# Tile-by-tile in place of pool-by-pool waits at the stage transitions of a transformer block

## The chip, the cores and the metric

The kernel runs on one core of one Trainium2 chip. The metric is device time in microseconds (us) of one execution, as the median of several executions; lower is better. The core has a matrix engine (TensorE, PE in the profile; its weight loads are the row PEld), a vector engine (DVE), an activation engine (ACT), POOL, and SP, which here issues all DMA transfers of the program (every issue on the page stands under SP). In the traces the engines work side by side and stand where they need each other's results (DVE stood 87.5 us in all for the snapshots of ACT, in the page of the kernel before); the built program does this with semaphores. Accumulators lie in PSUM, at the two last transitions in tiles of 128 x 512 float32 or of twice that; the down product's pool has eight of the former, which the built program puts into banks 0 to 7, one each. Everything else lies in SBUF or DRAM.

## The reference

Two sub-blocks behind each other, on 2048 tokens of width 1024, in bfloat16:

```python
x = A_x
h = x + A_ref(layernorm(x), A_wqkv, A_wo)        # linear attention, 32 heads of 32
h2 = h + B_ref(layernorm(h), W_gate, W_up, W_down)
# B_ref: gate = relu(x @ W_gate); up = x @ W_up; (gate * up) @ W_down, width 3584
```

## The kernel before

The kernel multiplies by Strassen's scheme with 7 block products (hence the sums called s, t, hs, tg, tu), and goes through stages: k, v and q products; attention interleaved with the rest of q and the first gate/up products; gate/up in a wide form with accumulators of two banks; the down product, in two halves s = 0 and s = 1. Each stage opens pools of tiles in memory that an earlier stage has closed. The pools at the two last transitions:

```python
    psctx.close()
    abctx.close()
    ps2ctx = ExitStack()
    ps2 = ps2ctx.enter_context(tc.tile_pool(name="ps2", bufs=1, space=PSUM))
    apools = [ps2, ps2ctx.enter_context(tc.tile_pool(name="ps2b", bufs=1, space=PSUM))]
    hhpool = ctx.enter_context(tc.tile_pool(name="hhpool", bufs=1, side="right"))
    prepool = ctx.enter_context(tc.tile_pool(name="prepool", bufs=1, side="right"))
    # ... (cut: the loop over the gate/up units)
            p1()
            if prev:
                prev()
            p2()
            prev = p3
    prev()
    ps2ctx.close()
    mctx.close()

    dpool = ctx.enter_context(tc.tile_pool(name="dpool", bufs=1))
    dwork = ctx.enter_context(tc.tile_pool(name="dwork", bufs=4))
    ps3 = ctx.enter_context(tc.tile_pool(name="ps3", bufs=8, space=PSUM))
```

One gate/up unit, with its three accumulators A, Dp and E. A comes from ps2 and ps2b in turn. `snap` is a copy on ACT; `finish_sum` is the drain of an accumulator, an addition on DVE (its line is L615):

```python
        def finish_sum(ps, m, q):
            gu = mwork.tile([P, 2, SW], BF16, tag="gu", name="gu")
            nc.vector.tensor_tensor(out=gu[:], in0=ps[:], in1=m[:], op=ALU.add)     # L615
            # ... (cut: relu on ACT, product on DVE, store of hh)

        def part1():
            st["A"] = A = apools[k % len(apools)].tile([P, 2, SW], FP32, tag="A", name="A")
            prod(A, 1, True)
            m1 = snap(A)
            Dp = ps2.tile([P, 2, SW], FP32, tag="D", name="Dp")
            prod(Dp, 2, True)
            finish_sum(Dp, m1, 0)

        def part2():
            A = st["A"]
            prod(A, 6, False)
            st["u2"] = snap(A)
            st["E"] = E = ps2.tile([P, 2, SW], FP32, tag="E", name="E")
            prod(E, 5, True)
            prod(A, 7, False)
            finish_sum(E, snap(A), 3)

        def part3():
            A, E = st["A"], st["E"]
            prod(A, 4, False)
            # ... (cut: relu and product of A)
            prod(E, 3, False)
            finish_sum(E, st["u2"], 1)
```

The start of the down product, which needs four one-bank accumulators at a time:

```python
        def prod(accs, lhs, rhs, start, after):
            for half in range(2):
                for tt in TT:
                    for f in range(FD):                                     # FD = 7
                        nc.tensor.matmul(accs[tt][:], ...)                  # L759
                    if half == 1:
                        after(tt)
        # ... (cut)
        accA = [ps3.tile([P, DW], FP32, tag="s", name="accA") for _ in TT]
        prod(accA, h11, b11, True, after(lambda tt: snap(accA[tt], 0, tt, "m1"), m1))

        s3 = h21[:].bitcast(FP16)
        for v in range(2):
            fs = slice(v * FD, (v + 1) * FD)
            nc.vector.tensor_tensor(out=s1[:, fs], in0=h21[:, fs], in1=h22[:, fs], op=ALU.add)
            nc.vector.tensor_tensor(out=s2[:, fs], in0=s1[:, fs], in1=h11[:, fs], op=ALU.subtract)
            nc.vector.tensor_tensor(out=s3[:, fs], in0=h11[:, fs], in1=h21[:, fs], op=ALU.subtract)
        accD = [ps3.tile([P, DW], FP32, tag="s", name="accD") for _ in TT]
        prod(accD, h12, b21, True, after(lambda tt: store(0, tt, accD[tt], m1[tt])))
        # ... (cut: sums t1, t2, then the product of s2 and t2 into accA, and so on)
```

## Time and profile before

| | before |
|---|---|
| time, median of 3 runs | 769.52 us (768.56 to 771.18) |
| profiled span | 768.0 us |
| PE busy | 740.3 us, 96% |
| DVE busy | 482.0 us, 63% |

The busy times from the page of the kernel before (engine, us, share of the span, number of instructions):

```profile
PE 740.3 (96%) x3584; PEld 340.2 (44%) x3584; DVE 482.0 (63%) x868; ACT 321.6 (42%) x593; POOL 6.1 (1%) x44
```

Busy for 96% of the span, PE is what bounds the kernel, so the question for any wait is whether PE stands in it. The timeline of PE before shows where it stood at the two last transitions and in the down product. Columns: start in us, length, engine, source line, what is written and read, how many; in brackets the idle time before and what ended it.

```profile
586.91 1.03 PE L596 MATMUL A<-hn,tu 128*128 128x512 f16 x4
589.03 1.02 PE L596 MATMUL A<-hn,tg 128*128 128x512 bf16 x4 [1.10 <-ACT snap L610]
...
591.62 1.03 PE L596 MATMUL E<-hs,wu 128*128 128x512 f16 x4
594.06 12.25 PE L759 MATMUL accA<-wd,hh 128*128 128x512 bf16 x56 [1.41 <-DVE gu L615]
...
711.12 6.20 PE L759 MATMUL accA<-t,s 128*128 128x512 f16 x28 [0.57 <-DVE t L822]
```

Taken as idle time, these are the only three stops over 0.3 us from 298 us on. The one at 594.06 is the transition from gate/up (L596) to the down product (L759). The chain of waits before, around it (start, us, what), says what PE waited for:

```profile
590.92 1.74 PE E L596 x8
592.66 0.02 issue
592.69 1.24 DVE gu L615
593.92 0.14 issue
594.06 12.25 PE accA L759 x56
```

DVE drained E, the last accumulator of gate/up, for 1.24 us, and only then did the first matmul of accA start, 0.14 us later. But accA does not read E. It waited because its pool lies in the memory of a closed pool.

### The profile page before, as it was taken

To read this page: it belongs to the slowest core of one execution; us is meant where nothing else is said; L and a number is where in the kernel's file an instruction comes from. 1 tells how busy PE (TensorE), PEld (TensorE's weight loads), DVE (VectorE), ACT (ScalarE), POOL (GpSimd) and SP (SyncE) were. 2 spreads that over 40 slices of the span, in tenths; PEclk is the share of its full clock that TensorE was granted. 3 is DMA by queue.
4 is the path that set the end of the run, shared out by engine and by line. 5 is a ranking of instruction groups with operands and counts; after the bars stand their busy time and mean duration, and the time that the engine had idled before them with its cause. 6 is when DMAs were issued, how large, how long until landed. Compare 5 with 4: busy or idle time off the path is not lost.

```text
span 768.0 us, 9610 instructions
## 1 busy us (share of the span) xinstructions
PE 740.3 (96%) x3584; PEld 340.2 (44%) x3584; DVE 482.0 (63%) x868; ACT 321.6 (42%) x593; POOL 6.1 (1%) x44
## 2 busy tenths in 40 slices
PE   5999999999889999999999999999998999999998
PEld 2444555444344444444444444444443444444443
DVE  5997654886896766656474564746545991349632
ACT  4775553877777554444444344444434000000000
POOL 0000000000000000000000000000000000000000
PEclk9999999999999999999999999999999999999999
DMA  9675003089767526154032140130001986971001
GB/s 321 145 138 150 1 1 110 1 186 225 180 154 192 121 63 209 45 152 131 7 87 72 34 131 8 55 103 29 28 7 60 331 261 209 316 256 49 28 27 55
DMA packets 125151, 89.76 MB, mean 117 GB/s; under 512 B 50352, under 2 KB 116912, under 8 KB 124592
## 3 DMA queue, kind: packets, MB, share of 16 engines
q1 hardware_dynamic: 125104, 89.15, 40.9%
q8 instruction: 28, 0.46, 0.2%
q14 instruction: 19, 0.16, 0.1%
HBM read 59.77 MB, written 17.83 MB: 101 GB/s over the span
## 4 chain that ended last, share of the span: by engine, by line
PE 64%; DVE 20%; ACT 8%; DMA 4%; issue 3%; SPq 0%; POOL 0%; DVEq 0%; ACTq 0%
PE A L596 16%; PE accA L759 11%; PE E L596 8%; PE accE L759 6%; PE attn L514 4%; DVE gu L615 4%; PE Aq L280 3%; PE Dp L596 3%; PE Aq L414 2%; PE Eq L280 2%; ACT snap L610 2%; PE Aq L629 2%; PE accD L759 2%; DVE stats L249 2%; DMA hn<-hn 1%
## 5 line engine op out<-in xcount | busy, mean ns | idle before, releaser
L615 DVE TENSOR_TENSOR gu<-E,snap 128x1024 bf16<-128x1024 f32 x48 | 58.7, 1223 | 90.1 <-ACT snap L610 87.5
L610 ACT COPY snap<-A 128x1024 f32<-128x1024 f32 x72 | 72.0, 1008 | 84.1 <-PE A L596 84.1
L759 PEld LDWEIGHTS <-hh 128*128 128x128 bf16 (+1 forms) x560 | 54.7, 98 | 67.7 <-issue 1.9
L617 ACT ACTIVATE gu<-gu 128x512 bf16<-128x512 bf16 x72 | 45.4, 630 | 86.2 <-DVE gu L615 85.9
L759 PE MATMUL accA<-wd,hh 128*128 128x512 f16 (+1 forms) x336 | 73.3, 379 | 1.4 <-DVE gu L615 1.4
L514 PE MATMUL attn<-wo_mem,oT 128*128 128x512 bf16 x256 | 59.3, 385 | 3.4 <-DVE o_sb L494 3.1
L596 PEld LDWEIGHTS <-tg 128*128 128x128 f16 x384 | 37.5, 98 | 49.5 <-issue 5.7
L596 PEld LDWEIGHTS <-tu 128*128 128x128 f16 x384 | 37.6, 98 | 45.3
L618 DVE TENSOR_TENSOR hh<-gu 128x512 bf16<-128x512 bf16 x72 | 30.5, 423 | 38.4 <-ACT gu L617 38.4
L147 ACT COPY u<-Aq 128x512 f32<-128x512 f32 x56 | 32.2, 581 | 44.5 <-PE Aq L280 20.9
L596 PE MATMUL A<-hn,tg 128*128 128x512 f16 (+1 forms) x192 | 49.3, 379 | 1.1 <-ACT snap L610 1.1
L596 PE MATMUL A<-hn,tu 128*128 128x512 f16 (+1 forms) x192 | 49.3, 379 | 0.0
L596 PEld LDWEIGHTS <-wg 128*128 128x128 bf16 x288 | 28.2, 98 | 34.5 <-issue 1.1
L596 PEld LDWEIGHTS <-wu 128*128 128x128 bf16 x288 | 28.2, 98 | 34.0
L514 PEld LDWEIGHTS <-oT 128*128 128x128 bf16 x256 | 25.2, 99 | 36.0 <-issue 8.6
L759 PEld LDWEIGHTS <-s 128*128 128x128 f16 x224 | 21.9, 98 | 27.2 <-issue 0.8
L615 DVE TENSOR_TENSOR gu<-Dp,snap 128x1024 bf16<-128x1024 f32 x24 | 29.3, 1220 | 2.3 <-PE Dp L596 2.3
L280 PEld LDWEIGHTS <-xT 128*128 128x128 bf16 (+1 forms) x192 | 18.6, 98 | 23.9 <-issue 2.4
L767 DVE TENSOR_TENSOR u<-accA,hres 128x512 f32<-128x512 f32 x16 | 10.8, 690 | 28.6 <-PE accA L759 28.1
L494 DVE TENSOR_TENSOR o_sb<-nd,rd 128x384 bf16<-128x384 f32 (+1 forms) x48 | 22.9, 508 | 8.6 <-ACT rd L493 8.3
L516 DVE SCALAR_TENSOR_TENSOR x_res<-attn,x_res 128x512 bf16<-128x512 f32 x32 | 22.0, 688 | 7.7 <-PE attn L514 7.6
L596 PE MATMUL E<-hs,tg 128*128 128x512 f16 x96 | 24.6, 378 | 0.9
(161 smaller groups left out, 1217.5 us busy)
## 6 DMA issues: line engine op xcount, KB each, us to landing
wd<-in_B_W_down_dram SPq DMA_DIRECT2D x16, 896.0 KB, 6.5
hh_dram<-hh SPq DMA_DIRECT2D x72, 128.0 KB, 1.7
wg<-in_B_W_gate_dram SPq DMA_DIRECT2D x14, 512.0 KB, 4.9
wu<-in_B_W_up_dram SPq DMA_DIRECT2D x14, 512.0 KB, 4.9
hh<-hh_dram SPq DMA_DIRECT2D x4, 1792.0 KB, 8.0
x_sb<-in_A_x_dram SPq DMA_DIRECT2D x16, 256.0 KB, 3.8
x_res<-in_A_x_dram SPq DMA_DIRECT2D x16, 256.0 KB, 3.0
h_dram<-x_res SPq DMA_DIRECT2D x16, 256.0 KB, 2.6
```

Source lines behind the costliest of these rows:

```text
L147: nc.scalar.copy(out=snaps[nm, v], in_=A[v][:])
L249: nc.vector.bn_stats(out=stats[:, k, :], in_=x_sb[:, k * NW:(k + 1) * NW])
L280: nc.tensor.matmul(ps[:], lhsT=left[m - 1][:, kc, r + v * P:r + (v + 1) * P], rhs=right[m - 1][:, kc, :], start=(start and kc == 0), stop= ...
L494: nc.vector.tensor_tensor(out=ov[:, c0:c0 + n], in0=ndv[:, :, 0:P].rearrange("p k (h e) -> p k h e", h=HPC), in1=rd[:, 0:n, :].unsqueeze(3 ...
L514: nc.tensor.matmul(ps[:], lhsT=st["oT"][:, c, :], rhs=wo_sb[:, c, j * NW:(j + 1) * NW], start=(c == 0), stop=(c == KC - 1))
L516: nc.vector.scalar_tensor_tensor(out=h_sb[:, j * NW:(j + 1) * NW], in0=ps[:], scalar=1.0, in1=h_sb[:, j * NW:(j + 1) * NW], op0=ALU.mult, ...
L596: nc.tensor.matmul(ps[:, v, :], lhsT=w[v][m - 1][:, kc, :], rhs=left[m - 1][:, kc, :], start=(start and kc == 0), stop=(kc == KH - 1), ski ...
L610: nc.scalar.copy(out=m[:], in_=ps[:])
L615: nc.vector.tensor_tensor(out=gu[:], in0=ps[:], in1=m[:], op=ALU.add)
L617: nc.scalar.activation(out=gu[:, 0, :], in_=gu[:, 0, :], func=ACT.Relu)
L618: nc.vector.tensor_tensor(out=d, in0=gu[:, 0, :], in1=gu[:, 1, :], op=ALU.mult)
L759: nc.tensor.matmul(accs[tt][:], lhsT=lhs[:, half * FD + f, tt * P:(tt + 1) * P], rhs=rhs[half][:, f, :], start=(start and half == 0 and f ...
```

## The change

The intent is that a pool opened in memory of earlier pools no longer waits until all of these are done with. Each of its tiles waits for the users of its own bytes. It is one argument on each pool opened at a transition, on 14 lines in all; the core of the diff:

```diff
-    abpool = abctx.enter_context(tc.tile_pool(name="abpool", bufs=3, space=PSUM, side="right"))
+    abpool = abctx.enter_context(tc.tile_pool(name="abpool", reuse_waits="tile", bufs=3, space=PSUM, side="right"))
# ... (cut: the same for qwork0, qwork1, aops, wpool, tpool, mwork)
-    ps2 = ps2ctx.enter_context(tc.tile_pool(name="ps2", bufs=1, space=PSUM))
+    ps2 = ps2ctx.enter_context(tc.tile_pool(name="ps2", reuse_waits="tile", bufs=1, space=PSUM))
# ... (cut: the same for ps2b, hhpool, prepool, dpool, dwork)
-    ps3 = ctx.enter_context(tc.tile_pool(name="ps3", bufs=8, space=PSUM))
+    ps3 = ctx.enter_context(tc.tile_pool(name="ps3", reuse_waits="tile", bufs=8, space=PSUM))
```

Comparing the two built programs shows that no instruction is added, removed or moved on any engine, apart from those that only wait. At the start of accA the waits change like this (the number is the semaphore value waited for; DVE 747 is the drain of E; DVE 746 is the last read of A by DVE, which ended 0.4 us before that drain began; ACT 575 is the last read of A by ACT):

```
before                                      after
wait alone            DVE 747               -
weights of accA tt=0  POOL 40               no wait
matmul of accA tt=0   ACT 575               no wait
first matmul of tt=3  -                     DVE 746
first matmul of accD tt=1  -                DVE 747
```

The banks of the built program say why: accA's four tiles lie in banks 0, 7, 6 and 5, accD's in 4, 3, 2 and 1. Dp was in 0 and 1, E in 2 and 3, the last A in 4 and 5, the A before it in 6 and 7. Only the second accD tile (bank 3) meets E.

More of the change, by code (lines that the diff above doesn't have):

```diff
@@ L424, in q_unit @@
         return strassen(pspool, qw[-1], mm, fin)
-    with tc.tile_pool(name="qwork0", bufs=2, side="right") as pool:
+    with tc.tile_pool(name="qwork0", reuse_waits="tile", bufs=2, side="right") as pool:
         qw.append(pool)
@@ L432, in block_kernel @@
     q1ctx = ExitStack()
-    qw.append(q1ctx.enter_context(tc.tile_pool(name="qwork1", bufs=2, side="right")))
+    qw.append(q1ctx.enter_context(tc.tile_pool(name="qwork1", reuse_waits="tile", bufs=2, side="right")))
     mctx = ExitStack()
@@ L441, in new_hn @@
     def new_hn(s):
-        aops = mctx.enter_context(tc.tile_pool(name=f"aops{s}", bufs=1))
+        aops = mctx.enter_context(tc.tile_pool(name=f"aops{s}", reuse_waits="tile", bufs=1))
         hnT.append([aops.tile([P, KC, SW], BF16, name=f"hn{s}{i}") for i in range(2)])
@@ L448, in block_kernel @@
     NE = 2 * GP
-    wpool = mctx.enter_context(tc.tile_pool(name="wpool", bufs=2))
+    wpool = mctx.enter_context(tc.tile_pool(name="wpool", reuse_waits="tile", bufs=2))
     wg_v = wg.rearrange("(kc p) (h f) -> p kc h f", p=P, h=2)
@@ L566, in block_kernel @@
     new_hn(1)
-    tpool = mctx.enter_context(tc.tile_pool(name="tpool", bufs=2))
-    mwork = mctx.enter_context(tc.tile_pool(name="mwork", bufs=2))
+    tpool = mctx.enter_context(tc.tile_pool(name="tpool", reuse_waits="tile", bufs=2))
+    mwork = mctx.enter_context(tc.tile_pool(name="mwork", reuse_waits="tile", bufs=2))
     hh0 = []
@@ L704, in block_kernel @@
     ps2ctx = ExitStack()
-    ps2 = ps2ctx.enter_context(tc.tile_pool(name="ps2", bufs=1, space=PSUM))
-    apools = [ps2, ps2ctx.enter_context(tc.tile_pool(name="ps2b", bufs=1, space=PSUM))]
-    hhpool = ctx.enter_context(tc.tile_pool(name="hhpool", bufs=1, side="right"))
-    prepool = ctx.enter_context(tc.tile_pool(name="prepool", bufs=1, side="right"))
+    ps2 = ps2ctx.enter_context(tc.tile_pool(name="ps2", reuse_waits="tile", bufs=1, space=PSUM))
+    apools = [ps2, ps2ctx.enter_context(tc.tile_pool(name="ps2b", reuse_waits="tile", bufs=1, space=PSUM))]
+    hhpool = ctx.enter_context(tc.tile_pool(name="hhpool", reuse_waits="tile", bufs=1, side="right"))
+    prepool = ctx.enter_context(tc.tile_pool(name="prepool", reuse_waits="tile", bufs=1, side="right"))
     hh0 += [hhpool.tile([P, FH, SW], BF16, tag="hh", bufs=4, name="hh") for q in range(4)]
@@ L736, in block_kernel @@
     mctx.close()
-    dpool = ctx.enter_context(tc.tile_pool(name="dpool", bufs=1))
-    dwork = ctx.enter_context(tc.tile_pool(name="dwork", bufs=4))
-    ps3 = ctx.enter_context(tc.tile_pool(name="ps3", bufs=8, space=PSUM))
+    dpool = ctx.enter_context(tc.tile_pool(name="dpool", reuse_waits="tile", bufs=1))
+    dwork = ctx.enter_context(tc.tile_pool(name="dwork", reuse_waits="tile", bufs=4))
+    ps3 = ctx.enter_context(tc.tile_pool(name="ps3", reuse_waits="tile", bufs=8, space=PSUM))
     TT = range(NT)
```

## The prediction

> **What bounds the kernel now.** TensorE. The page gives PE 740.3 us busy of 768.0 (96%), granted clock 1.0 nearly everywhere; DVE has 63%. [...] in the timeline matmuls of 512 columns start every 0.216 us, and from 298 us to the last start at 763.8 us that rhythm breaks visibly only three times: 1.3 us at 589.0 (a snapshot that the last gate/up unit's next product needs), 1.57 us at 594.06 (the step from gate/up to the down product) and 0.7 us at 711.1 (a weight sum on DVE).
>
> **What the change does.** No instruction is added, removed or reordered on any engine; only wait conditions change. By stage transition:
>
> 1. Attention's q work and first gate/up tiles (about 125 to 205 us). Some waits go from PE, ACT, POOL and the DMA queue. None of the idle PE time there ends with one of them: the waits view names DVE results that are data (pq_mem, o_sb, x_res, 1 to 2 us each). Worth 0.
> 2. Gate/up with the wide accumulators (297.8 us). The first matmul no longer waits for all earlier PE work; the timeline shows no gap. Worth 0.
> 3. Down product (594.06 us). Before, accA's first matmul waited for the last DVE addition out of the old accumulators, ACT and POOL. The chain of waits shows: matmuls of E end 592.66, DVE gu 592.69 to 593.92, 0.14 us of passing on, accA 594.06. After, the first accA bank has no such wait; the wait moves to the fourth token tile's first matmul (for a DVE result of 592.3) and to accD (for the addition that ends at 593.92), needed about 597 and 607. So PE goes straight on: start to start falls from 1.79 to 0.22 us, saving 1.57 us, all on the critical path.
>
> **Does it survive?** The loads of wd keep their place in the queue behind the hh stores, so the second half of the first weight block still is issued at about 592.7 and lands at 597.7. PE will want it 28 matmuls after its start, at 592.5 + 6.05 = 598.5: about 0.8 us to spare. The hres loads lose a wait for a store (issued 601.5, after about 597), but DMA is full there (share about 1.0 from 595 to 613), so they land hardly sooner. The tightest DVE result is the first half of t (ready 616.1, needed from about 616.7). The gap at 711 should stay about 0.6 us. So I keep 1.5 us.
>
> **Predicted time.** 769.52 - 1.5 = 768.0 us, range 766.2 to 769.8 (the runs before spread 2.6 us). Faster by over 2%: 0.005; within 2%: 0.99; slower: 0.005.
>
> **What would show it.** In the chain of waits DVE gu no longer stands between E and accA; in the timeline accA starts about 0.2 us after E's last start; the idle time "PE accA <- DVE gu 1.4" leaves the groups; hres issues move 4 us forward; nothing before 592 us moves by 0.3 us; span about 766.5.
>
> **What would make it wrong.** The second wd half arriving after 598.5, so that the gap returns 6 us later as a wait for DMA; t late by some tenths at 617; the 711 us gap growing; or an earlier hidden wait among the SBUF pools that the profile puts down to another engine (another 1 to 2 us before 300 us).

## The result, and the profile after

| | before | after |
|---|---|---|
| first comparison, median (runs) | 769.04 us (4) | 767.48 us (4) |
| ratio of the fast runs, 95% interval | | 0.9981 (0.9962 to 0.9999) |
| profiled span | 768.0 us | 767.3 us |
| last start of E to first start of accA | 1.79 us | 0.22 us |
| first wide gate/up matmul to the end | 470.18 us | 468.48 us |

A ratio compares the fast runs of one kernel with those of the other, so it is not quite the ratio of the medians quoted. By the bar of 2% the time is the same.

The chain of waits after, at the same place:

```profile
590.05 1.89 PE A L596 x8
591.94 1.73 PE E L596 x8
593.67 12.09 PE accA L759 x56
605.75 12.09 PE accD L759 x56
617.84 12.09 PE accA L759 x56
```

The drain of E is no longer in the chain. The timeline after shows it running beside accA:

```profile
592.64 1.03 PE L596 MATMUL E<-hs,wu 128*128 128x512 f16 x4
593.29 4.63 PEld L759 LDWEIGHTS <-hh 128*128 128x128 bf16 x22
593.50 4.70 PE L759 MATMUL accA<-wd,hh 128*128 128x512 bf16 x21
593.71 1.23 DVE L615 TENSOR_TENSOR gu<-E,snap 128x1024 bf16<-128x1024 f32 x1 [0.41 <-PE E L596]
```

The two other stops are still there:

```profile
590.05 1.02 PE L596 MATMUL A<-hn,tg 128*128 128x512 bf16 x4 [1.10 <-ACT snap L610]
```

and the stop at 711 us before is a start-to-start distance of 0.94 us at 710.57 after (0.95 before).

At the last gate/up products this profile is 1.02 us later than the one before. That is not the change. The two programs have the same waits up to the first q matmul, which already came at 125.97 against 125.09 us; from there to the first wide gate/up matmul both took about the same, 172.87 and 172.71 us. The first wide gate/up matmuls, before and after:

```profile
297.81 1.03 PE L596 MATMUL A<-hn,wg 128*128 128x512 bf16 x4
298.84 1.03 PE L596 MATMUL A<-hn,wg 128*128 128x512 bf16 x4
```

So comparisons below use the stretch from the first wide gate/up matmul to the end of the span, which holds the two last transitions and whose start is the same point in every kernel.

### The profile page after: what moved, and what is told of

Read it like the earlier page. It is cut to its first block, busy times and chain, and to the rows that moved or that the text cites. A ratio compares the mean times of both kernels' runs of the same rounds, so it can differ in the third digit from the quotient of the medians.

```text
span 767.3 us, 9604 instructions
## 1 busy us (share of the span) xinstructions
PE 740.9 (97%) x3584; PEld 340.4 (44%) x3584; DVE 481.8 (63%) x868; ACT 321.8 (42%) x593; POOL 6.2 (1%) x44
## 4 chain that ended last, share of the span: by engine, by line
PE 66%; DVE 19%; ACT 7%; DMA 5%; issue 3%; SPq 0%; DVEq 0%; ACTq 0%
PE A L596 16%; PE accA L759 10%; PE E L596 8%; PE accE L759 6%; PE attn L514 5%; PE Aq L280 4%; DVE gu L615 4%; PE Dp L596 3%; PE Aq L414 2%; PE Eq L280 2%; PE Aq L629 2%; ACT snap L610 2%; DVE stats L249 2%; PE accD L759 2%; DMA hn<-hn 1%
```

## The experiments

The theory: the whole gain is PE's stop before accA, removed because the first three accA tiles lie in banks that were drained long before. Rivals: the gain comes from loads that start earlier (the SBUF pools); it comes from many small waits; it comes from having fewer waits at all, wherever the banks lie; the DMA or DVE chain soon takes it back.

The parts of the span, all worked out from the starts in the traces, in us. "Half clock" tells whether the granted TensorE clock fell to 0.5 for 3.41 us near 206 us in that execution (more on this below).

| profile of | start to first q | first q to first wide gate/up | half clock | first wide gate/up to end | last E to accA |
|---|---|---|---|---|---|
| before | 125.09 | 172.71 | yes | 470.18 | 1.79 |
| after | 125.97 | 172.87 | yes | 468.48 | 0.22 |
| e1, after again | 127.04 | 172.73 | yes | 468.49 | 0.22 |
| e2, ps3 alone | 125.05 | 171.30 | no | 468.59 | 0.22 |
| e3, all but ps3 | 126.59 | 171.49 | no | 469.95 | 1.70 |
| e4, E in first banks | 124.63 | 171.55 | no | 469.93 | 1.70 |
| e6, the same again | 124.09 | 171.54 | no | 469.94 | 1.69 |
| e7, gap filled | 125.13 | 172.93 | yes | 467.19 | - |
| e8, and s3 later | 125.15 | 171.45 | no | 466.49 | - |
| e9, before, control | 126.32 | 171.56 | no | 470.16 | 1.79 |
| e10, after | 125.56 | 171.47 | no | 468.48 | 0.22 |
| e11, before, control | 126.32 | 171.62 | no | 470.18 | 1.79 |
| e12, after | 125.60 | 171.69 | no | 468.59 | 0.22 |

Eight of the profiles (e1 to e4, e9 to e12) lack 60 of the 3584 matmul records; those that the table rests on are there.

The last stretch has two parts that differ between the kernels. One is the last column. The other is the tail, from the last matmul's start to the end of the span: 4.20 to 4.23 us in the four profiles whose SBUF pools keep the old waits (before, e2, e9, e11), and 4.07 to 4.11 us in the nine others. This 0.12 us comes among the closing instructions of the program (L884), after the last store has landed; why is not shown. The rest of the stretch is the same to 0.03 us in all profiles but e7 and e8, which change it, and e12 (0.13 us more).

### e1: the whole change again

The edit: none; the changed kernel.

> The whole change again, beside the others on one chip. My theory (one PE wait of 1.57 us at the step to the down product is all of it): ratio to before 0.9980, that is 1.5 us less; accA starts 0.22 us after the last start of E, and no other start of PE moves against its neighbours by over 0.3 us. Rival 'many small waits at all transitions': the same total, but spread over several steps of PE's timeline.

Measured: median 768.79 us against 769.73, ratio 0.9986 (0.9973 to 0.9999). The stretch to the end was 468.49 us, as in the first profile. The ratio expected, 0.9980, lies inside that interval. One expectation was missed in this profile: starts before 300 us moved against their neighbours by up to 1.6 us (a transpose at 10.5 us came 3.31 us after the one before it, against 1.72 us), all of it ahead of the first wait that the change touches.

### e2: the new waits for ps3 alone

```diff
-    ps3 = ctx.enter_context(tc.tile_pool(name="ps3", bufs=8, space=PSUM))
+    ps3 = ctx.enter_context(tc.tile_pool(name="ps3", reuse_waits="tile", bufs=8, space=PSUM))
# nothing else of the change
```

> The kernel before with the new waits for the PSUM pool of the down product (ps3) alone; hres and the other loads keep their old waits. My theory: all of the gain, 1.5 us (ratio 0.9980); accA 0.22 us after E; hres still issued about 4 us later than in the changed kernel. Rival 'the SBUF pools give the gain, by loads that start earlier': no gain, ratio 1.000, and the 1.4 us gap before accA stays.

Measured: 768.59 us against 769.73, ratio 0.9986 (0.9972 to 1.0). The chain of waits of e2:

```profile
589.45 1.73 PE E L596 x8
591.18 7.55 PE accA L759 x35
```

There is no drain between E and accA, and the stretch to the end is 468.59 us, within 0.11 us of the whole change. The hres loads of this kernel kept their late place: they were issued 8.9 us after the last E matmuls' end (600.10 against 591.18 us), as before (601.51 against 592.66). So the pool of the down accumulators alone gives the 1.57 us before accA, without any earlier load. The 0.11 us that are left are the tail, which is the old one here (4.20 against 4.09 us).

### e3: all but ps3

```diff
-    ps3 = ctx.enter_context(tc.tile_pool(name="ps3", reuse_waits="tile", bufs=8, space=PSUM))
+    ps3 = ctx.enter_context(tc.tile_pool(name="ps3", bufs=8, space=PSUM))
# the rest of the change stays
```

> The changed kernel with ps3 alone put back to waiting pool by pool; some fifteen pools keep the new waits. My theory: no gain, ratio 1.000 within 0.001, the gap before accA back at 1.57 us (start to start 1.79), though hres is issued about 4 us earlier. Rival 'SBUF pools': the gain stays, 0.998.

Measured: 770.23 us against 769.73, ratio 1.0008 (0.9996 to 1.0021). The chain of waits of e3:

```profile
591.18 1.74 PE E L596 x8
592.92 0.02 issue
592.94 1.24 DVE gu L615
594.18 0.05 issue
594.23 7.73 PE accA L759 x35
```

The stop is back though all the other pools keep the new waits, and the hres loads went out at 597.33 us, 4.4 us after the end of E in place of 8.9. The rival of the SBUF pools falls: the loads do start earlier, and PE's stop is not shorter for it. One small thing is seen here: the drain's end reaches PE in 0.05 us, not 0.14. The program before had three waits at this point, one of them an instruction of its own; this one has two, on the weight load and the matmul themselves. That is part of the 0.23 us by which this stretch (469.95) is under before (470.18): 0.09 us of it. Most of the rest, 0.13 us, is the shorter tail.

### e4 and e6: E in the banks that the first accA tile gets

```diff
-    ps2 = ps2ctx.enter_context(tc.tile_pool(name="ps2", reuse_waits="tile", bufs=1, space=PSUM))
+    psE, ps2 = (ps2ctx.enter_context(tc.tile_pool(name=n, reuse_waits="tile", bufs=1, space=PSUM)) for n in ("psE", "ps2"))
-            st["E"] = E = ps2.tile([P, 2, SW], FP32, tag="E", name="E")
+            st["E"] = E = psE.tile([P, 2, SW], FP32, tag="E", name="E")
# the rest of the change stays
```

This puts E into banks 0 and 1 and Dp into 2 and 3. No instruction is added or removed, but accA's first tile, in bank 0, now lies on E, and its first matmul waits for DVE 747.

> The changed kernel with all its tile-by-tile waits, but the accumulator E of gate/up, the last one that is drained, lies in PSUM banks 0 and 1 in place of 2 and 3, so that the first accA tile, which gets bank 0, lies on it. If the gain is that the first tile's own bytes happen to be free (my theory), the gap of about 1.57 us before accA comes back in full and the ratio to before is 1.000, with nothing else changed. Rival 'tile-by-tile waits as such, or the fewer wait instructions, give the gain': 0.998 as in the whole change.

> The kernel with E in the banks that the first accA tile gets, again, because its first five rounds did not tell 1.000 from 0.998 though its trace had the gap back. If the gap costs what the trace shows, then among runs of full clock it is 1.4 to 1.5 us slower than the whole change beside it, and 0.1 us faster than before; from the first wide gate/up matmul to the end 469.95 us again. If the gap were repaid elsewhere, that stretch would be near 468.5.

Measured: e4 768.01 us against 769.73, ratio 0.9987 (0.9972 to 1.0002); e6 768.48 against 768.57, ratio 0.9998 (0.9984 to 1.0013). The chain of waits of e6:

```profile
588.73 1.74 PE E L596 x8
590.47 0.02 issue
590.49 1.24 DVE gu L615
591.73 0.04 issue
591.77 8.36 PE accA L759 x38
```

The stop is back, at 1.70 and 1.69 us start to start, with every tile-by-tile wait in place, and the stretch to the end is 469.93 and 469.94 us, against 468.5. So it is not the kind of wait that gains, but that under it the first tiles needed lie where nobody works any more. By time alone the matter was less clear. The ratio of e4, expected at 1.000, came out like those of e1 and e2 beside it. Runs at full clock averaged 768.39 us (11 runs, both sets), which lies between the pooled 768.85 of before and 767.58 of after, nearer to before but not by an amount that these runs could hold against their scatter. The expectation that e6 would be 1.4 to 1.5 us slower than the run of the whole change beside it was missed (768.61 against 767.87 us at full clock, 6 and 3 runs).

### e5: the whole change a third time

> The whole change a third time, as the yardstick for the three kernels beside it. From the first matmul of gate/up's wide stage to the end of the span 468.5 us (before 470.2). Ratio to before 0.998; single runs scatter by about 1.5 us, by whether the TensorE clock fell to half for 3.4 us near 206 us (mean clock 0.997 or 0.998 then, 0.999 or 1.0 otherwise).

Measured: 768.73 us median, ratio 0.9998 (0.9981 to 1.0015), a miss. The profiled execution fell in the slow state: 978.14 us, with a mean granted clock of 0.755. It is left out of the ratio, of the table and of every comparison, and so the stretch expected at 468.5 us could not be checked here. With 0.9981 and 0.9986 before, this third ratio raised the question whether something takes back half of the gain; e9 to e12 answer it.

### e7: the next stop filled

The stop at 589 us is PE's wait for a snapshot of A, which has no other work to hide it since the last unit has no successor. Tile-by-tile waits allow a pool to take over the two drained banks of the other A before gate/up has ended, so seven matmuls of the down product can be put there:

```diff
             prev = p3
+    ps2bctx.close()
+    psx = ctx.enter_context(tc.tile_pool(name="psx", reuse_waits="tile", bufs=2, space=PSUM, side="right"))
+    # spare(): two tiles of psx; accX = spare()
+    for f in range(FD):
+        nc.tensor.matmul(accX[0], lhsT=hh0[0][:, f, 0:P], rhs=first_wd[0][:, f, :], start=(f == 0), stop=False, ...)
     prev()
     ps2ctx.close()
# ps3 has 6 tiles; accA of s = 0 and accD, accE of s = 1 take two of theirs from psx;
# ps2b stands on the other side of PSUM; both halves of the first weight block are loaded early (prepool bufs=2)
```

> The whole change, and the 1.26 us hole before the last gate/up product (at 589 us) filled with the first seven matmuls of the down product, into a PSUM pool that takes over the two banks of the accumulator that is already drained; the second half of the first weight block is loaded early as well, so that its landing (0.7 us ahead of its use in the changed kernel) does not become the next wait. Theory that PE's own starts bound the time here: the stretch from the first wide gate/up matmul to the end falls by a further 1.1 to 1.3 us, to 467.3. Rival 'the DMA or DVE chain behind it takes over': the hole goes, and a wait of about the same size comes at the product of s2 and t2.

Measured: 767.7 us against 768.57, ratio 0.9986 (0.9971 to 1.0001); five of its six runs had a mean clock of 0.998 or less, as with the half clock stretch, against one of the eleven of before, so this ratio probably understates the gain. The timeline of PE in e7:

```profile
587.14 1.03 PE L596 MATMUL A<-hn,tu 128*128 128x512 f16 x4
588.00 1.67 PE L744 MATMUL accX<-wd,hh 128*128 128x512 bf16 x7
589.51 1.03 PE L596 MATMUL A<-hn,tg 128*128 128x512 bf16 x4
```

No idle time stands in brackets any more, and the stretch to the end fell to 467.19 us, 1.29 under the whole change (1.26 was the hole). Nothing came in its place at the product of s2 and t2: from 560 us on, the stop near 709 us is the only one left over 0.15 us. The rival, a DMA or DVE chain that takes over, falls for this stretch.

### e8: the last stop as well

```diff
-            nc.vector.tensor_tensor(out=s3[:, fs], in0=h11[:, fs], in1=h21[:, fs], op=ALU.subtract)   # was in the loop of s1, s2
# in the down product, behind the loop that makes t1 and t2:
+        for v in range(2):
+            fs = slice(v * FD, (v + 1) * FD)
+            nc.vector.tensor_tensor(out=s3[:, fs], in0=h11[:, fs], in1=h21[:, fs], op=ALU.subtract)
# on top of e7
```

> The kernel with the hole filled, and the two DVE sums s3 put behind the sums t1 and t2, which the product before needs: the 0.73 us wait of PE for t in the second half (at 711 us) should go. The stretch from the first wide gate/up matmul to the end 466.6 us, 1.9 us under the whole change and 3.6 under before; ratio to before about 0.9955.

Measured: 765.22 us (763.95 to 767.16) against 768.57, ratio 0.9956 (0.994 to 0.9971). The stretch to the end is 466.49 us. This beats both kernels (though not by the bar of 2%), and PE has no stop left over 0.15 us between 560 us and its last matmul:

```profile
699.64 11.39 PE L773 MATMUL accA<-t,s 128*128 128x512 f16 x52
710.86 3.18 PE L773 MATMUL accX<-wd,s 128*128 128x512 f16 x14
```

### e9 to e12: control and change side by side

The edit: none, twice the kernel before and twice the changed kernel.

> The kernel before against itself: shows what the time and the parts of the span scatter with nothing changed. Expected: ratio 1.000, interval about 0.0013 wide to each side; start to the first q matmul anywhere from 124 to 127 us, from there to the first wide gate/up matmul 171.0 to 171.5 (1.2 to 1.4 us more with the half clock near 206 us), from there to the end 470.2. If start to q keeps to about 125.1 here and to 126 to 127 in the whole change, the timed gain is smaller than 1.6 us for a reason that lies in the first stage.

> The whole change a fourth time, beside that control. Expected: ratio 0.998 (the three sets so far: 0.9981, 0.9986, 0.9998); first wide gate/up matmul to the end 468.5; start to q 124 to 127 as in the control, as up to there the two programs are the same.

> The control once more, for a second profile of it: as the first control.

> The whole change a fifth time, for one more profile of it: as the fourth. All sets together should give 1.2 to 1.7 us less than before; if they give 0.7 or less, something that the traces do not show takes back half of the gain.

Measured, against the same runs of before (770.05 us median): the controls 0.9993 (0.9979 to 1.0006) and 0.9987 (0.9973 to 1.0), the whole change 0.9976 (0.996 to 0.9992) and 0.9973 (0.996 to 0.9986). The second control shows that the same kernel can come out 0.13% under itself, with an interval that just holds 1. The traces show where times scatter: the first q matmul came anywhere from 124.09 to 127.04 us in the thirteen fast profiles, in a stage whose program is the same in all of them, and neither kernel has the early or the late times for itself (before 125.09, 126.32, 126.32; after 125.97, 127.04, 125.56, 125.60). The stretch behind it is the same to 0.4 us apart from the half clock (171.56 and 171.62 us in the controls, a little over the 171.0 to 171.5 expected), and the stretch from the first wide gate/up matmul on repeats to 0.03 us for before and 0.11 us for after.

All sets together, fast runs that list their clock, mean time in us:

| | mean clock 0.999 or 1.0 | clock 0.998 or less (taken for runs with a half clock stretch) |
|---|---|---|
| before | 768.85 (33 runs) | 770.17 (12) |
| after | 767.58 (18) | 769.06 (9) |
| difference | -1.27 | -1.11 |

With standard deviations of about 0.8 us per run the first difference is good to about 0.5 us, counting the scatter of single runs alone. But the sets ran on different chips: set by set, at full clock, it was 0.36 us (e1), 0.70 us (e5) and 1.87 us (e9 to e12), from 3 to 18 runs a side. It is compatible with the 1.57 us of the trace; it does not measure it better than the trace does. The last expectation, 1.2 to 1.7 us in all, held at full clock and was narrowly missed in the other column; nothing was found that takes half of the gain back.

## Why the prediction was right

- **What bounds the kernel.** Right. Removing stops of PE moved the end of the span by their size, three times: 1.57, then 1.26, then 0.73 us, where the stretch to the end fell by 1.70 (0.12 of it the tail), 1.29 and 0.70 us. PE busy was 740.3 us before and 740.9 after, so the busy time did not show the change. The distances between starts did (1.79 to 0.22 us).
- **Point 1, attention and q, worth 0.** Right. First q to first wide gate/up took 171.56 and 171.62 us in the controls and 171.47 and 171.69 us in the change, all without half clock.
- **Point 2, start of the wide gate/up, worth 0.** Right: from the first wide gate/up matmul to the last start of E it took 294.46 us before and 294.45 after.
- **Point 3, 1.57 us at the down product.** Right in place and size: start to start 1.79 to 0.22 us. e2 shows that ps3 alone gives it, e3 that the other pools do not, e4 and e6 that the bank of the first tile decides. The 0.12 us of the tail came on top and was not predicted.
- **Does it survive.** Right in what came out, with two numbers to correct. The second half of the first weight block landed at 598.88 us and its first matmul was due at 593.50 + 28 x 0.216 = 599.55 us, so 0.67 us were to spare (predicted 0.8). The hres loads were issued 4.4 us earlier and landed no sooner: measured against the end of E, 11.6 us after it in both kernels (604.29 and 605.30 us). But the wd loads behind them did land sooner, the first of them 1.4 us (609.43 before; 609.07, less the shift of 1.02, after), and so t was ready at 615.76 us for a use at 617.68 us: 1.9 us to spare in place of the 0.6 that I had called the tightest place. I had taken the old DVE times as fixed.
- **The time.** 768.0 us predicted, with 766.2 to 769.8; the first comparison gave 767.48, later sets 768.79, 768.73, 767.87 and 767.68. The range would also have held the unchanged kernel (769.04 in the same comparison), so the time alone says nothing for the mechanism; the traces of e2 to e4 and e6 do.
- **What would show it.** Two of the signs were badly chosen, "nothing before 592 us moves by 0.3 us" and "span about 766.5". The last gate/up products moved by 1.02 us, and the span was 767.3, by scatter that I had not looked for in one profile. A sign should have been a distance between two events on either side of the change.

## What to carry to other kernels

Here relaxing the waits of a pool opened in the memory of a closed one paid only where PE, which bounds the kernel, stood at the transition: 1.57 us at the down product, nothing measurable between the first q and the first wide gate/up matmul (171.56 and 171.62 us before, 171.47 and 171.69 after). And there the first tile needed counted: 0.22 us start to start with its bank free, 1.70 and 1.69 us with it on the last buffer to be drained (e4, e6). So look at both: where the bounding engine stands, and whether the bytes of its first tile lie on that buffer. A change of two tenths of a per cent was measured in the trace, as the distance between two events that frame it, which repeated to 0.03 us for before and 0.11 us for after; timed runs of this kernel scatter by about 0.8 us (standard deviation), and a control of the kernel against itself, which came out at 0.9993 and 0.9987, tells how far to believe them. Once a wait is gone, list the next stops of the same engine: here two more, found in the same list, gave 1.29 and 0.70 us, together more than the change (1.70 us).

## What else the traces showed

- The clock. Four of thirteen fast profiles (before, after, e1, e7) had a stretch of 3.41 us at a granted clock of 0.50 near 206 us. In it, before and after, 512-column matmuls started 0.43 us apart, against 0.216 us at a granted clock of 1.00. In the 3.41 us ahead of it PE was busy for 1.21 us before, 1.15 after and 1.41 in e1. But little work of PE there does not tell these executions from the others: in e3 PE was busy for only 1.31 us of the 4 us from 204 to 208 us, and its clock stayed at 1.00 from 200 to 220 us. The line of the window view of before (stretch: length, PE, PEld, DVE, ACT and POOL busy, granted clock, DMA share, GB/s) for the stretch ahead and the stretch itself:

```profile
202.39:205.80 3.41, 1.21 (x7) 0.36 (x5) 3.41 (x12) 3.41 (x11) 0.00 (x0) 1.00 0.44 117
205.80:209.20 3.40, 2.91 (x7) 0.98 (x7) 2.50 (x6) 1.27 (x6) 0.00 (x0) 0.50 0.60 155
```

  With it the stretch between first q and first wide gate/up was 1.3 us longer in the mean (172.81 against 171.52 us), and runs with a low mean clock were 1.3 to 1.5 us longer. What made the clock fall is not shown.
- The passing on of a wait. In the kernel before, with one wait instruction of its own and two more waits, the drain's end took 0.14 us to reach PE; with one or two waits and no such instruction it took 0.04 to 0.05 us (e3, e6).
- The scatter of identical programs. Here the first stage ended anywhere from 124.09 to 127.04 us; the stretch behind it repeated to 0.4 us at full clock, and the last one to 0.11 us.
- The slow execution of e5. It took 978.14 us at a mean granted clock of 0.755. Why is not shown.
